# A retention and mixture-of-adapters kernel: the first half unit's scores moved into the last full unit, PSUM banks given to the state update first in the first chunk, one transposed key tile copied batch by batch

## The chip, the cores and the metric

The kernel runs on one core of a Trainium2 chip. The metric is the device time of one execution in microseconds. A core has five engines that work side by side and wait for one another through semaphores: TensorE (matrix products and transposes, its weight loads are listed apart in the profile), VectorE, ScalarE, GpSimd, and SyncE, which here issues most transfers. Matrix products land in PSUM, eight banks of which one holds 512 float32 values per partition.

## The reference, cut to what matters

Retention of 8 batches with 8 heads, sequence 576 and head dimension 64, then a mixture of 8 low-rank adapters of rank 16, of which each token uses two:

```
scores = scale * q @ k.T
out    = (scores * Dmat[h]) @ v          # Dmat = gamma_h ** (i - j) for j <= i, else 0
x      = out as (batch*seq, heads*64)    # 4608 x 512
logits = x @ w_gate; top 2 of 8, softmax weights w
result = x + sum over the two: w * (x @ A[e]) @ B[e]
```

## The kernel before, in words

The sequence is cut into four chunks of 128 positions and a last one of 64. A *unit* is one chunk of two batches: units 0 to 15 are full, 16 and 17 are the half chunk, each with four batches (two by two). Units 0 to 3 belong to the first chunk, which has no state from earlier chunks; from unit 4 on a state `P` (one tile for each pair of batches) carries the earlier chunks. The loads fetch four batches at a time (`q32`, `k32`, `v32`, three sets of buffers), so one load serves two units.

The work on a unit is split into stages, each a function:

- `stage_T` transposes q and k on TensorE into the PSUM tiles `pqT`, `pkT` (two each, one for each half of the positions) and copies them to `qT`, `kT` in SBUF, by VectorE in the first units and by ScalarE otherwise. `scale_k` then weights k in place on GpSimd (line 261).
- `stage_S` makes the scores, two PSUM tiles `ps` for each batch of a full unit, and VectorE multiplies each by the decay mask into `rt`. A half unit has two score tiles `pe` and results `rh`.
- `stage_Q` takes two tiles `px` and, where there is a state, adds `P` times `qT` into them. For a first-chunk unit it only takes the two banks and returns.
- `stage_U` forms the state update `pu` from k and v (32 matmuls recorded). VectorE makes `P` (first chunk) or `pn` out of it, and GpSimd then writes `P`.
- `stage_R` adds v times `rt` into `px`; VectorE scales the result into `xT`.
- `stage_Z` multiplies `xT` by the adapters and the gate into `pz`; VectorE copies the logits to `lg` and makes `ns`. `stage_V` runs the sigmoids `sg` on ScalarE (called by `stage_W` where it has not run), `stage_W` makes the weights `cm` and the weighted `zc` on VectorE and gives the bank of `pz` back.
- `stage_B` transposes `xT` back into two tiles `po`, `stage_X` transposes `zc` (`pzt`, copied to `zT`), and `stage_Y` adds the adapters' output to `po`, copies it to `osb` and stores it.

Three things set the order around the change. First, the matmuls, VectorE's and ScalarE's instructions are each chained in the order in which the stages are called (`chain`, lines 73 to 87, which is why nearly all of them carry line 81, 84 or 87 in the profile); GpSimd's and SyncE's are put in order by the framework. Second, the loop at the end (lines 607 to 708) interleaves stages of neighbouring units: a full unit t from 3 on runs S, T of unit t+1, W and B of unit t-1, Q, U, R, then X, Z and Y. Third, the PSUM banks are handed out by a queue:

```
def bank(shape, name, dtype=FP32):
    n = free.pop(0)
    ...
def done(*tiles):
    free.extend(held.pop(id(x))[0] for x in tiles)
```

A bank goes to the back of the queue when the *program text* gives it back, which may be right after the reading instruction was written down. A later tile that gets the same bank waits, at run time, until the last reader of the tile before it has finished. So the order in which `bank` is called decides which reader a tile waits for.

## Time and profile before

| | us |
|---|---|
| median of 4 runs | 195.03 |
| the runs | 195.12, 194.94, 194.85, 196.33 |
| time of the profiled execution | 195.12 |
| its span | 193.3 (mean granted TensorE clock 0.988) |
| TensorE matmuls busy | 180.6 |
| weight loads busy | 163.5 |
| VectorE busy | 110.4 |
| ScalarE busy | 72.0 |
| GpSimd busy | 58.8 |

A row of the timeline gives the start and the duration in microseconds, the engine (PE is TensorE's matmuls, PEld its weight loads, DVE VectorE, ACT ScalarE, POOL GpSimd), the line, the operation, "written tile <- read tiles", the shapes, how many instructions are merged into the row, and in brackets how long the engine had been idle and who the profile thinks released it. A matmul of float32 appears as two records, so a stage of 16 matmuls shows as 32. The releaser is inferred from semaphores; where an instruction waits for several, or where two engines signal at nearly the same time, the name can be wrong. A releaser "issue" means that the profile shows no wait.

### The profile page before, as it was taken

The numbers are of one execution on the slowest core, as the hardware profiler recorded it, in microseconds if no ns is written. First come the engines' busy times: TensorE is split into PE (matmuls) and PEld (weight loads), VectorE is DVE, ScalarE is ACT, GpSimd is POOL, SyncE is SP. The second block draws the span as 40 slices with busy tenths as digits, with TensorE's granted clock in tenths as the row PEclk, the third lists the DMA queues.
The fourth block names the chain that finished last, engine by engine and source line by source line (L and its number), as shares of the span: only waits on it lengthen the run. The fifth ranks groups of instructions, "written<-read, shape, count | busy, mean of one in ns | idle before, by whom it ended". The sixth has DMA issues, their size and how long they took to land. (4 is left out here: it accounts for less than half of the span.)

```text
span 193.3 us, 8113 instructions
## 1 busy us (share of the span) xinstructions
PE 180.6 (93%) x3612; PEld 163.5 (85%) x3612; DVE 110.4 (57%) x281; ACT 72.0 (37%) x195; POOL 58.8 (30%) x70
## 2 busy tenths in 40 slices
PE   7799997999999999979999999999999999988870
PEld 2598997989999999979999999999999999978750
DVE  4476956565656574744646564646474746453650
ACT  4111154262616170705252525344443435070440
POOL 8984026040424233330606051514242420200000
PEclk9999999999999999999999999999999999999995
DMA  6999978997998999696889898949980302020343
GB/s 138 266 242 251 288 221 234 249 300 216 254 369 252 240 335 270 172 283 225 231 242 304 264 259 229 251 110 244 186 209 1 114 3 112 3 112 3 112 109 109
DMA packets 53746, 38.73 MB, mean 200 GB/s; under 512 B 27472, under 2 KB 49104, under 8 KB 53712
## 3 DMA queue, kind: packets, MB, share of 16 engines
q1 hardware_dynamic: 52736, 37.75, 69.5%
q8 instruction: 28, 0.46, 1.0%
q10 hardware_dynamic: 832, 0.34, 0.6%
q0 software_dynamic: 144, 0.13, 0.4%
q14 instruction: 6, 0.05, 0.1%
HBM read 28.91 MB, written 9.44 MB: 198 GB/s over the span
## 5 line engine op out<-in xcount | busy, mean ns | idle before, releaser
L261 POOL TENSOR_TENSOR k<-k,pack 128x512 f32<-128x512 f32 x32 | 32.7, 1042 | 81.8 <-PE pkT L81 71.3
L84 DVE TENSOR_TENSOR rt<-ps,mask 128x512 f32<-128x512 f32 x64 | 41.0, 686 | 16.5 <-PE ps L81 15.7
L81 PE MATMUL pz<-AW,xT 128*128 128x136 f32 x288 | 37.4, 283 | 0.2 <-DVE xT L84 0.2
L81 PE MATMUL ps<-qT,kT 64*128 64x128 f32 x512 | 35.7, 281 | 0.9 <-DVE kT L84 0.9
L81 PEld LDWEIGHTS pz<-AW,xT 128*128 128x128 f32 x288 | 34.6, 190 | 0.6 <-DVE xT L84 0.5
L81 PEld LDWEIGHTS ps<-qT,kT 64*128 64x128 f32 x512 | 31.0, 188 | 4.0 <-PE po L81 2.7
L81 PE MATMUL px<-rt,v 128*64 128x128 f32 x512 | 31.0, 273 | 1.1 <-issue 1.1
L87 ACT COPY osb<-po 128x256 f32<-128x256 f32 x68 | 20.6, 386 | 28.4 <-PE po L81 28.0
L84 DVE TENSOR_TENSOR xT<-px,asc 128x512 f32<-128x512 f32 x36 | 24.6, 691 | 9.3 <-PE px L81 8.2
L81 PEld LDWEIGHTS px<-rt,v 128*64 128x64 f32 x512 | 27.9, 137 | 1.2 <-issue 1.2
L87 ACT COPY zT<-pzt 128x256 f16<-128x256 f16 (+1 forms) x19 | 6.9, 361 | 54.1 <-PE pzt L81 54.1
L87 ACT COPY kT<-pkT 128x512 f32<-128x512 f32 x33 | 17.9, 590 | 14.7 <-PE pkT L81 14.7
L395 POOL TENSOR_TENSOR P<-pn,gdec 128x512 f32<-128x512 f32 x12 | 15.3, 1272 | 25.5 <-DVE pn L84 22.6
L87 ACT COPY qT<-pqT 128x512 f32<-128x512 f32 x32 | 17.2, 590 | 8.3 <-PE pqT L81 8.3
L81 PE MATMUL pu<-v,k 128*64 128x64 f32 x512 | 18.4, 225 | 1.6 <-POOL k L261 1.1
L81 PEld LDWEIGHTS pu<-v,k 128*64 128x64 f32 x512 | 16.3, 138 | 4.1 <-issue 2.6
L84 DVE COPY lg<-pz 128x16 f32<-128x16 f32 (+1 forms) x19 | 3.3, 173 | 26.6 <-PE pz L81 26.6
L84 DVE TENSOR_TENSOR pn<-pu,P 128x512 f32<-128x512 f32 x12 | 8.3, 692 | 16.0 <-PE pu L81 16.0
L81 PE MATMUL px<-qT,P 64*64 64x128 f32 (+1 forms) x512 | 15.9, 262 | 0.6 <-issue 0.6
L81 PEld LDWEIGHTS px<-qT,P 64*64 64x64 f32 x512 | 12.7, 133 | 1.7 <-issue 0.7
L81 PE MATMUL po<-id,xT 64*128 64x64 f32 x288 | 12.7, 224 | 0.7 <-DVE zc L84 0.7
L81 PE MATMUL pkT<-id,k 64*128 64x64 f32 x288 | 12.4, 224 | 0.6 <-DMA k<-in_k_dram 0.5
(51 smaller groups left out, 149.6 us busy)
## 6 DMA issues: line engine op xcount, KB each, us to landing
out_dram<-osb SPq DMA_DIRECT2D x32, 256.0 KB, 3.1
q<-in_q_dram SPq DMA_DIRECT2D x4, 512.0 KB, 6.5
k<-in_k_dram SPq DMA_DIRECT2D x4, 512.0 KB, 7.2
v<-in_v_dram SPq DMA_DIRECT2D x4, 512.0 KB, 7.6
out_dram<-osb SPq DMA_DIRECT2D x6, 128.0 KB, 2.3
Arow<-in_moe_A_dram SPq DMA_DIRECT2D x1, 256.0 KB, 5.4
out_dram<-osb ACTq DMA_DIRECT2D x2, 128.0 KB, 2.7
Bcat<-in_moe_B_dram POOLq DMA_DIRECT2D x1, 128.0 KB, 4.7
```

The lines of the kernel that those rows point to most:

```text
L81: chain("pe", nc.tensor.matmul(*args, **kw))
L84: chain("dve", getattr(nc.vector, fn)(**kw))
L87: chain("act", getattr(nc.scalar, fn)(**kw))
L261: gp.tensor_tensor(out=kk[:, b], in0=kk[:, b], in1=gv[:, 0].unsqueeze(2).broadcast_to((128, H, Dh)), op=ALU.mult,)
L395: nc.gpsimd.tensor_tensor(out=Pt, in0=pn, in1=gdec, op=ALU.mult)
```

## The change

Three edits, and no instruction is added except two copies:

1. In the first chunk (units 0 to 3) `stage_U` is called before `stage_Q`. As `stage_Q` there only takes two banks, TensorE's order stays the same: U, then R. What changes is that `pu` now takes the first free bank and `px` the next two, where `px` took the first two and `pu` the third.
2. In unit 15, the last full one, `stage_S` of unit 16 is called between `stage_Q` of unit 15 and `stage_Q` of unit 16, where before it opened unit 16. TensorE runs Q(15), S(16), Q(16), U(15), R(15), X(14), Z(15), Y(14), and then goes straight on to the transposes of unit 17; VectorE makes `rh` of unit 16 before `pn` of unit 15. The banks of the tiles in between move with it: `pe` takes the banks that `px` of unit 16 took, `px` of unit 16 those of `pkT` of unit 16, `pu` of unit 15 that of the first `pe`.
3. In unit 0, `kT` is copied in four pieces, one for each half of the positions and each batch (ScalarE takes one half, VectorE the other), where it was two whole tiles. The scores of batch 0 then need only the first two pieces.

```diff
-                if t < 2 and nm == "qT" or t < 3 and nm == "kT" and g == 1:
+                if t == 0 and nm == "kT":
+                    for b in range(2):
+                        x = dst[:, b, :, rows(g)]
+                        if g == 1:
+                            vec("tensor_copy", out=x, in_=ps[g][:, :, b])
+                        else:
+                            act("copy", out=x, in_=ps[g][:, :, b])
+                elif t < 2 and nm == "qT" or t < 3 and nm == "kT" and g == 1:
                     vec("tensor_copy", out=o, in_=ps[g])
...
+            stage_U(0)
             stage_Q(0)
-            stage_U(0)
             stage_R(0)
...
+            stage_U(1)
             stage_Q(1)
-            stage_U(1)
             stage_R(1)
...
+            stage_U(2)
             stage_Q(2)
-            stage_U(2)
             scale_k(3)
             stage_R(2)
...
             stage_B(t - 1)
-            stage_Q(t)
+            if units[t][0] > 0:
+                stage_Q(t)
             if not is_full(t + 1):
+                stage_S(t + 1)
                 stage_Q(t + 1)
             stage_U(t)
             scale_k(t + 1)
+            if units[t][0] == 0:
+                stage_Q(t)
             stage_R(t)
...
-        stage_S(t)
         stage_W(t - 1)
         stage_T(t + 1)
```

## The prediction

> **What bounds the kernel now.** I read the page first (busy shares, slices, granted clock), then the timeline of TensorE with the idle time ahead of each group, then the waits and the neighbours of each hole. The chain that ended last covers only the last 2 us, so I don't use it.

> ```profile
> span 193.3 us, 8113 instructions
> ...
> PE 180.6 (93%) x3612; PEld 163.5 (85%) x3612; DVE 110.4 (57%) x281; ACT 72.0 (37%) x195; POOL 58.8 (30%) x70
> ...
> PEclk9999999999999999999999999999999999999995
> ...
> q8 instruction: 28, 0.46, 1.0%
> ```

> TensorE works 180.6 of 193.3 us at full clock; no other engine is near that. The program only gets shorter where TensorE stands still. The holes that the change can touch, from the timeline:

> ```profile
> 8.90 2.06 PE L81 MATMUL ps<-qT,kT 64*128 64x128 f32 x32 [0.91 <-DVE kT L84]
> ...
> 16.08 0.71 PE L81 MATMUL pkT<-id,k 64*128 64x64 f32 x16 [0.48 <-DMA k<-in_k_dram]
> ...
> 30.18 2.48 DVE L84 TENSOR_TENSOR rt<-ps,mask 128x512 f32<-128x512 f32 x4 [1.31 <-PE ps L81]
> ...
> 31.65 2.04 POOL L261 TENSOR_TENSOR k<-k,pack 128x512 f32<-128x512 f32 x2 [1.58 <-PE pkT L81]
> ...
> 32.77 1.15 PE L81 MATMUL pu<-v,k 128*64 128x64 f32 x32 [1.13 <-POOL k L261]
> ...
> 42.23 1.15 PE L81 MATMUL pu<-v,k 128*64 128x64 f32 x32 [0.47 <-DVE cm L84]
> ...
> 85.80 0.44 PE L81 MATMUL px<-rt,v 128*64 128x128 f32 x4 [1.07 <-issue]
> ```

> ```profile
> 161.59 1.07 ACT L87 COPY kT<-pkT 128x512 f32<-128x512 f32 x2 [0.36 <-PE pkT L81]
> ...
> 161.94 2.37 PE L81 MATMUL px<-qT,P 64*64 64x128 f32 x96
> ...
> 162.52 0.48 DVE L84 TENSOR_TENSOR zc<-pz,cm 128x128 f16<-128x128 f32 x2
> ...
> 169.52 1.20 ACT L87 COPY osb<-po 128x256 f32<-128x256 f32 x4 [1.75 <-PE po L81]
> 169.63 1.02 PEld L81 LDWEIGHTS pe<-qT,kT 64*64 64x64 f32 x64 [0.21 <-PE po L81]
> ...
> 170.57 0.52 ACT L87 ACTIVATE sg<-lg,ns 128x8 f32<-128x8 f32 x2
> ...
> 170.84 1.29 DVE L84 TENSOR_TENSOR rh<-pe,maskh 128x512 f32<-128x512 f32 x2 [0.90 <-PE pe L81]
> ...
> 172.05 0.35 DVE L84 SCALAR_TENSOR_TENSOR cm<-pz,m,sg 128x8 f32<-128x8 f32 x2
> ...
> 172.85 0.71 PE L81 MATMUL po<-id,xT 64*128 64x64 f32 x15 [0.39 <-DVE zc L84]
> ...
> 176.11 0.34 PE L81 MATMUL px<-qT,P 64*64 64x64 f32 x7 [0.60 <-issue]
> ```

> Between 45 and 160 us the only hole is the one at 85 us.

> **U first (units 0 to 3).** Walking the free list through the program tells whose bank each tile inherits. In unit 2, pu takes the bank of the fourth ps tile; its reader is the fourth rt operation, which ends at 32.66, and U starts at 32.73. The row names GpSimd's scaling, but that pair scales unit 3's k, and its second half ends at 33.69 while U's second head, which waits for its own k half, loads at 32.85: the named releaser cannot be it. After the change pu takes the second ps bank, free at 31.47 (second of four operations from 30.18; they start 0.60 apart and take 0.69). The last transpose of kT is issued at 31.41, so U starts near 31.54: 1.19 earlier. Behind it, R's px banks are the third and fourth ps (free at 32.07 and 32.66); R begins 0.93 after U (32.47), its second half at 33.36, so neither waits. VectorE must still do cm and zc (to 33.33) before P, so P ends and xT starts at 33.82 where R would have allowed 33.64; Z then starts at 34.57 instead of 35.67. **1.1 us.**
> In unit 3, pu inherits the fourth ps again (rt ends at 42.08, U starts 42.20); afterwards it inherits pqT of unit 4, copied by ScalarE until 40.97. B ends at 41.61, the hole goes: **0.53** (0.47 and 0.58 on the two rows of the hole). R's fourth-ps bank (42.08) is needed only at 43.5. Units 0 and 1 show no wait at U (12.03 and 20.76 follow their predecessors), so they get 0. From unit 4 on every tile inherits a bank of the same role as before.

> Is the 1.6 us kept? Only a landing could eat it. The tightest is the third k transfer, landed at 38.94, wanted at 40.48 before and at 39.38 after: 0.4 us of cover. The three batches of buffers let it be issued without a wait for TensorE, so it doesn't move; if it came 1.5 us later, unit 2's gain would be gone. The second v landed at 29.78, wanted at 31.54; later transfers have 6 us and more.

> **kT by batch (unit 0).** Pieces of 256 elements instead of 512: the osb copies of 128x256 took 386 ns on ScalarE and 420 on VectorE, kT itself 590 and 684. First pieces end at 8.49 instead of 8.76, so S starts 0.27 earlier; the second pieces (8.86 at the latest) are wanted at 9.57. [...] But the 0.27 is worth **0**: TensorE reaches unit 1's kT transposes that much earlier and stands before a k transfer that landed at 15.95 (row at 16.08; the hole grows from 0.48 to some 0.75). If that cover is gone, it is 0.27 gained; pieces that fail to overlap lose at most 0.2, also hidden. ScalarE's AW copies and VectorE's rt follow in the same shade.

> **S and Q of unit 16 inside unit 15.** No instruction is added: 32 matmuls (64 weight loads, 1.02 us) and two rh operations move up, no DMA with them. S follows Q(15) at 162.86; kT's second copy has ended (162.67), but pe1 inherits pz(14), whose last zc ends at 163.00. TensorE resumed at 163.12 at that point before too, for px1 of Q(16), so this wait only changes its tenant. S ends at about 164.2, Q(16) (0.95) at 165.15. pu(15) now inherits pe0: rh0 runs from 164.3 to 164.97, just hidden; cover gone costs up to 0.1. U(15), R, X, Z and Y come 0.92 later than before. VectorE's pn and xT queue behind rh, which is done at 165.6, before pn is due at 166.4. ScalarE's order is unchanged.
> After Y(14) S is no longer there, and T(17) starts at 170.55 instead of 170.72. Then B(15) waits for zc(15): before, sg was over at 171.09 but cm stood behind rh on VectorE until 172.05. Now sg, behind the osb copies on ScalarE, runs 171.49 to 172.01, and zc ends 1.15 us after sg's start (unit 16: 179.29 to 180.44), at 172.64 instead of 172.80. TensorE just waits longer at the same place. **0.16 gained**, of 1.0 us that moved; between -0.1 and 0.3.

> **Code loading.** TensorE's program arrives in packets of 16 KB (28 packets, row q8), 256 instructions of 64 bytes. Counting TensorE's records, the "issue" holes that end at 85.80 and 176.11 (the last start before them is at 84.46 and 175.29) stand at records 3008 and 6848, fifteen blocks of 256 apart; the packets ahead of them landed at 84.58 and 174.91, and both times TensorE went on 1.2 us after the landing. [...] I take 0, range 0 to 0.2 while the packet starts on time. The two holes, 1.3 and 0.8 us from start to start, I leave where they are.

> **Sum** against the profiled execution (span 193.33, time 195.12, so 1.8 around it): 1.1 + 0.53 + 0 + 0.16 = 1.8; span 191.5, time 193.3. The median of the runs is 0.09 lower, within the rounding: **193.3 us**.

> **Rivals.**
> Rival 1. The new timing loses another code block. A packet started 3.8 us late at 79.6 to 83.4, when the DMA engines were nearly full; five other blocks last only 4.1 to 5 us. One more hole of 1.3: 194.6. Against: before's runs at 194.85 to 195.12 agree; for: one stands at 196.33.
> Rival 2. The same the other way, the hole at 85 goes: 192.0.
> Rival 3. The k landing holds unit 4, or the bank is not what U(2) waits for: 1.1 lost, 194.4. The order of VectorE's ends speaks against.
> [...]

> **How the numbers follow.** Chances: forecast 0.60 (own range 192.8 to 193.9), rival 1 0.14, rival 2 0.13, rival 3 0.08, rival 4 0.05. A measurement of this kernel can tell about 0.5% (1 us) from no change: faster means below 194.05. Faster: 0.59 of the forecast, all of rival 2, 0.02 of rival 3: 0.74. Same: 0.13 of rival 1, the rest of rival 3, 0.01 of the forecast: 0.20. Slower: rival 4, and 0.01 of rival 1 (two blocks lost): 0.06. The range, 191.9 to 194.8, takes in rivals 1 to 3; rival 4 is left out.

> **What would show it.** The pu groups of units 2 and 3 without a hole; pkT of unit 1 with some 0.75 us ahead of it; pe between two px groups near 163 us less 1.6, the wait there still 0.25; po(15) with 1.0 to 1.3 us ahead of it, for zc. Wrong: U(2) still held; a new "issue" hole of over 1 us, above all at 165 less 1.6; po(15) resumed later than 172.85 less 1.6.

## The result: 0.4% faster, half of what was forecast

The changed kernel takes **194.1 us** (median of 43 runs, 192.49 to 196.79); the kernel before, run beside it, takes 194.85 us (64 runs). The ratio is **0.9959** [0.9942 to 0.9975]. The forecast was 193.3 us, 1.7 us below the 195.03 that was known then; some 0.8 us came. The measured time lies inside the range (191.9 to 194.8), outside the likeliest case's own range (192.8 to 193.9), and the gain is under the 0.5% that separates "faster" from "same". In a later comparison the same kernel stood at 0.9943 [0.9921 to 0.9964], 193.55 us.

The profiled execution took 193.65 us (before: 195.12), with a span of 191.9 us (193.3). The page of the changed kernel:

```profile
span 191.9 us, 8118 instructions
...
PE 181.1 (94%) x3612; PEld 163.7 (85%) x3612; DVE 110.4 (58%) x282; ACT 72.0 (38%) x196; POOL 58.8 (31%) x70
...
PEclk9999999999999999999999999999999999999995
...
q8 instruction: 28, 0.46, 1.0%
```

TensorE's work (3612 matmuls), its clock (0.990 granted, 0.988 before) and the code packets (28) are as before; only idle time can have moved. The timeline of the changed kernel (start, duration, engine, line, operation, tiles, form, count, and in brackets the idle time ahead with its releaser):

```profile
9.00 0.65 ACT L87 COPY kT<-pkT 128x256 f32<-128x256 f32 x2 [5.13 <-PE pkT L81]
9.04 0.76 DVE L84 COPY kT<-pkT 128x256 f32<-128x256 f32 x2 [0.95 <-PE pkT L81]
...
9.61 2.06 PE L81 MATMUL ps<-qT,kT 64*128 64x128 f32 x32 [0.64 <-DVE kT L84]
...
16.08 0.67 PE L81 MATMUL pkT<-id,k 64*128 64x64 f32 x16
...
31.53 1.15 PE L81 MATMUL pu<-v,k 128*64 128x64 f32 x32
...
40.61 1.15 PE L81 MATMUL pu<-v,k 128*64 128x64 f32 x32
...
50.56 1.15 PE L81 MATMUL pu<-v,k 128*64 128x64 f32 x32
...
64.99 1.09 PE L81 MATMUL pz<-AW,xT 128*128 128x136 f32 x8 [0.37 <-issue]
...
160.52 1.29 PE L81 MATMUL pe<-qT,kT 64*64 64x64 f32 x61
...
161.66 1.15 PE L81 MATMUL px<-qT,P 64*64 64x64 f32 x61
...
163.37 0.27 PE L81 MATMUL px<-qT,P 64*64 64x64 f32 x2 [0.57 <-issue]
163.57 1.15 PE L81 MATMUL pu<-v,k 128*64 128x64 f32 x32
...
169.91 0.52 ACT L87 ACTIVATE sg<-lg,ns 128x8 f32<-128x8 f32 x2
170.28 0.41 DVE L84 SCALAR_TENSOR_TENSOR cm<-pz,m,sg 128x8 f32<-128x8 f32 x2 [1.00 <-ACT sg L87]
170.61 0.48 DVE L84 TENSOR_TENSOR zc<-pz,cm 128x128 f16<-128x128 f32 x2
171.24 0.68 PE L81 MATMUL po<-id,xT 64*128 64x64 f32 x15 [0.85 <-DVE zc L84]
...
174.66 0.35 PE L81 MATMUL px<-qT,P 64*64 64x64 f32 x9 [0.85 <-issue]
```

The two `pu` rows of units 2 and 3 have no bracket any more. The `pe` row of unit 16 stands between two `px` groups. But there are three "issue" holes where before had two: the one ahead of 85.80 is gone, a small one has come at 64.99, and a new one at 163.37 stands inside Q(16), between the moved S(16) and U(15).

How far each point of TensorE's timeline moved against the kernel before:

| start of | before, us | after, us | moved | since the row above |
|---|---|---|---|---|
| kT transposes, unit 1 | 16.08 | 16.08 | 0.00 | |
| U(2) | 32.77 | 31.53 | -1.24 | hole gone |
| U(3) | 42.23 | 40.61 | -1.62 | 0.2 given back at Z(2), 0.5 hole gone |
| Y (first `po<-Bcat` row after 65 us) | 67.00 | 65.91 | -1.09 | new hole at 64.99 |
| Y (first such row after 85 us) | 88.21 | 85.82 | -2.39 | before's hole at 85.80 not there |
| U(15) | 164.23 | 163.57 | -0.66 | S(16) ahead of it (0.83), new hole 0.8 |
| transposes of q, unit 17 | 170.72 | 168.97 | -1.75 | S(16) no longer here |
| B(15), second part | 172.85 | 171.24 | -1.61 | waits for `zc` |
| end of Q(17)'s hole | 176.11 | 174.66 | -1.45 | that hole is 0.2 longer |
| end of the span | 193.3 | 191.9 | -1.4 | |

So the two `pu` waits and the `zc` step gave about what was forecast. The middle hole was 0.8 us shorter here than before; what is missing is the hole at 163.37.

TensorE's instruction records (weight loads, matmuls and semaphore instructions, 7289 before and 7292 after), counted from the start, show what the "issue" holes are. Each of them stands directly behind a record whose number leaves the remainder 192 when divided by 256. There are 28 such places in either trace and 28 code packets, of 16384 bytes each, so such a place is taken for the border between two code blocks of 256 instructions (which makes 64 bytes each). From the traces, for the two late holes of the changed kernel and for the same two borders in the kernel before (times in us):

```
kernel  previous border passed  packet for the next block  block used up  TensorE goes on
before  6080 at 162.77          162.93 to 163.86           166.85         no hole
before  6592 at 173.09          173.87 to 174.91           175.29         176.11
after   6080 at 160.41          161.13 to 162.09           162.59         163.37
after   6592 at 171.42          172.17 to 173.42           173.60         174.66
```

In these four the packet for the next block starts 0.16 to 0.78 us after TensorE has passed the border into the current one and takes 0.9 to 1.25 us, and in the three with a hole TensorE goes on 1.2 to 1.3 us after it has landed. Where a packet had landed 1.24 us or more before the current block was used up, as nearly all do, the traces of this case show no hole; where it was under 1.17 us, each of them shows one. The block from 6080 to 6336 took 4.1 us before; with S(16) moved into it, it is used up in 2.2 us. Its packet started 0.72 us after the border here, not 0.16.

### The profile page after: what moved, and what is told of

It is laid out like the page before. It is cut to its first block, busy times and chain, and to the rows that moved or that the text cites. A ratio compares the mean times of both kernels' runs of the same rounds, so it can differ in the third digit from the quotient of the medians.

```text
span 191.9 us, 8118 instructions
## 1 busy us (share of the span) xinstructions
PE 181.1 (94%) x3612; PEld 163.7 (85%) x3612; DVE 110.4 (58%) x282; ACT 72.0 (38%) x196; POOL 58.8 (31%) x70
## 5 line engine op out<-in xcount | busy, mean ns | idle before, releaser
L261 POOL TENSOR_TENSOR k<-k,pack 128x512 f32<-128x512 f32 x32 | 32.7, 1042 | 78.8 <-PE pkT L81 73.5
L84 DVE TENSOR_TENSOR rt<-ps,mask 128x512 f32<-128x512 f32 x64 | 41.0, 686 | 16.2 <-PE ps L81 16.2
L81 PE MATMUL pz<-AW,xT 128*128 128x136 f32 x288 | 37.6, 283 | 0.6 <-issue 0.4
L81 PE MATMUL ps<-qT,kT 64*128 64x128 f32 x512 | 35.7, 281 | 0.6 <-DVE kT L84 0.6
L81 PEld LDWEIGHTS pz<-AW,xT 128*128 128x128 f32 x288 | 34.7, 190 | 1.2 <-DVE xT L84 0.5
L81 PEld LDWEIGHTS ps<-qT,kT 64*128 64x128 f32 x512 | 31.0, 188 | 3.7 <-PE po L81 2.7
L87 ACT COPY osb<-po 128x256 f32<-128x256 f32 x68 | 20.6, 386 | 29.1 <-PE po L81 26.9
L81 PE MATMUL px<-rt,v 128*64 128x128 f32 x512 | 30.8, 273 | 0.0
L84 DVE TENSOR_TENSOR xT<-px,asc 128x512 f32<-128x512 f32 x36 | 24.6, 690 | 7.7 <-PE px L81 6.6
L81 PEld LDWEIGHTS px<-rt,v 128*64 128x64 f32 x512 | 27.8, 137 | 0.0
L87 ACT COPY zT<-pzt 128x256 f16<-128x256 f16 (+1 forms) x19 | 6.9, 361 | 52.5 <-PE pzt L81 52.5
L87 ACT COPY kT<-pkT 128x512 f32<-128x512 f32 (+1 forms) x34 | 18.0, 579 | 14.7 <-PE pkT L81 14.6
L87 ACT COPY qT<-pqT 128x512 f32<-128x512 f32 x32 | 17.2, 592 | 8.1 <-PE pqT L81 8.1
L84 DVE COPY lg<-pz 128x16 f32<-128x16 f32 (+1 forms) x19 | 3.3, 173 | 26.8 <-PE pz L81 26.8
L81 PE MATMUL pu<-v,k 128*64 128x64 f32 x512 | 18.5, 225 | 0.0
L81 PEld LDWEIGHTS pu<-v,k 128*64 128x64 f32 x512 | 16.3, 138 | 2.3 <-issue 1.9
L81 PE MATMUL px<-qT,P 64*64 64x128 f32 (+1 forms) x512 | 16.1, 261 | 1.4 <-issue 1.4
L84 DVE TENSOR_TENSOR pn<-pu,P 128x512 f32<-128x512 f32 x12 | 8.3, 692 | 15.2 <-PE pu L81 15.2
L81 PEld LDWEIGHTS px<-qT,P 64*64 64x64 f32 x512 | 12.7, 133 | 2.5 <-issue 1.7
L81 PE MATMUL po<-id,xT 64*128 64x64 f32 x288 | 12.6, 224 | 1.1 <-DVE zc L84 1.1
L81 PEld LDWEIGHTS pqT<-id,q 64*128 64x128 f32 x288 | 11.4, 143 | 1.4 <-POOL pick L141 0.8
```

The source lines that it names most:

```text
L81: chain("pe", nc.tensor.matmul(*args, **kw))
L84: chain("dve", getattr(nc.vector, fn)(**kw))
L87: chain("act", getattr(nc.scalar, fn)(**kw))
L261: gp.tensor_tensor(out=kk[:, b], in0=kk[:, b], in1=gv[:, 0].unsqueeze(2).broadcast_to((128, H, Dh)), op=ALU.mult,)
```

## The experiments

The theory: the parts of the change are worth what the sum says, except that S(16) beside Q(15) and Q(16) makes one code block so short that its successor is late. The rivals: the move of S costs through waits of banks or VectorE; the U-first part or the kT part is worth less than summed; or it is only the random place of the code holes. All ratios are to the kernel before, run on the same chip in the same comparison (194.54 us in the first, 194.5 in the second, 194.35 in the third); nothing of the computation is left out in any of these kernels.

**U first alone.** The kernel before, with only

```diff
+            stage_U(0)
             stage_Q(0)
-            stage_U(0)
...
+            stage_U(1)
             stage_Q(1)
-            stage_U(1)
...
+            stage_U(2)
             stage_Q(2)
-            stage_U(2)
...
-            stage_Q(t)
+            if units[t][0] > 0:
+                stage_Q(t)
...
             stage_U(t)
+            if units[t][0] == 0:
+                stage_Q(t)
```

> U first in units 0 to 3 alone. Theory (the three edits add up, U first keeps its 1.6 us, and the moved scores of unit 16 give back about 0.6 through a code block that lands too late): 1.6 us below the kernel before, ratio 0.992; U of units 2 and 3 without a hole, T of unit 4 some 1.6 us earlier. Rival (holes from code blocks in the crowded middle eat about half of whatever TensorE gains before them, and the moved scores cost nothing): 0.8 us, ratio 0.996.

Measured: 193.15 us (14 runs), **0.9923** [0.9898 to 0.9949], a gain of 1.5 us. The timeline has both groups without a hole:

```profile
32.29 1.15 PE L81 MATMUL pu<-v,k 128*64 128x64 f32 x32
...
41.37 1.15 PE L81 MATMUL pu<-v,k 128*64 128x64 f32 x32
```

The profiled execution is the longest of the 14 (195.77 us), with code holes at 66, 125 and 177 us, so only its rows ahead of these are read here. This part is worth what the sum said (1.6 us), and it is as large as or larger than the gain of the whole change. Something in the other two parts takes from it.

**S(16) moved, alone.** The kernel before, with only

```diff
+                stage_S(t + 1)
                 stage_Q(t + 1)
...
-        stage_S(t)
```

> Scores of unit 16 inside unit 15 alone. Theory: a new hole of about 0.8 us between S and U, where the code block ends, less the 0.16 gained at B of unit 15: 0.6 us above the kernel before, ratio 1.003. Rival (it costs nothing): 0.16 below, ratio 0.999.

Measured: 195.1 us (22 runs), **1.0029** [1.0004 to 1.0054]: 0.6 us slower, where the prediction had this part at 0.16 us faster. Its timeline:

```profile
163.94 1.15 PE L81 MATMUL px<-qT,P 64*64 64x64 f32 x62
...
165.92 0.27 PE L81 MATMUL px<-qT,P 64*64 64x64 f32 x1 [0.83 <-issue]
166.12 1.15 PE L81 MATMUL pu<-v,k 128*64 128x64 f32 x32
```

The hole comes with this part alone, at the same record, 6336. The border before it was passed at 162.70, the packet ran from 163.37 to 164.54, the block was used up at 164.87, and TensorE went on at 165.92.

**kT by batch, alone.**

```diff
+                if t == 0 and nm == "kT":
+                    for b in range(2):
+                        x = dst[:, b, :, rows(g)]
+                        if g == 1:
+                            vec("tensor_copy", out=x, in_=ps[g][:, :, b])
+                        else:
+                            act("copy", out=x, in_=ps[g][:, :, b])
-                if t < 2 and nm == "qT" or t < 3 and nm == "kT" and g == 1:
+                elif t < 2 and nm == "qT" or t < 3 and nm == "kT" and g == 1:
```

> kT of unit 0 in four pieces alone. Theory: S of unit 0 starts 0.27 us sooner after the transposes, and TensorE waits that much longer for the k transfer of unit 1: 0, ratio 1.000. Rival (the early gain is kept): 0.27 below, ratio 0.9986; too small to tell by time, so the hole ahead of unit 1's kT transposes decides: about 0.75 us by the theory, 0.48 by the rival.

Measured: 194.69 us (22 runs), **1.0000** [0.9977 to 1.0024]. The scores of unit 0 do start sooner after their transposes:

```profile
9.45 2.06 PE L81 MATMUL ps<-qT,kT 64*128 64x128 f32 x32 [0.64 <-DVE kT L84]
```

The hole is 0.64 us instead of 0.91. That the 0.27 us is lost again ahead of unit 1's kT transposes could not be read here: the first loads landed some 0.8 us later in this execution, and there was no wait at that place at all. The interval allows a gain of 0.27 us (0.14%) as well as none.

The three parts add up to 0.9923, 1.0029 and 1.0000, or -0.48% together; the whole change measured -0.41% and -0.57%. Within the intervals they add up, and the S part is the one that had the wrong sign.

**S(16) out of the dense block.** The changed kernel, with S(16) after R(15) instead of between Q(15) and Q(16). It stays ahead of X, Z and Y, so the `zc` step keeps its gain:

```diff
-                stage_S(t + 1)
                 stage_Q(t + 1)
             stage_U(t)
...
             stage_R(t)
+            if not is_full(t + 1):
+                stage_S(t + 1)
```

> The changed kernel, but with the scores of unit 16 behind R of unit 15 instead of between the two Q. The same work then leaves the code block that ends in the dense stretch 1.9 us longer. Theory: no hole between Q of unit 16 and U of unit 15, 1.7 us below the kernel before, ratio 0.991. Rival (the hole has another cause, such as the wait of pe on zc, or U on the bank of pe): a hole stays where pe is written, or comes back as a wait of equal size; ratio 0.995 to 0.996 as in the changed kernel.

Measured: 192.96 us (22 runs), **0.9917** [0.9896 to 0.9937]. The timeline:

```profile
159.64 2.36 PE L81 MATMUL px<-qT,P 64*64 64x128 f32 x96
161.93 1.15 PE L81 MATMUL pu<-v,k 128*64 128x64 f32 x32
...
164.76 1.16 PE L81 MATMUL pe<-qT,kT 64*64 64x64 f32 x64
...
170.69 0.68 PE L81 MATMUL po<-id,xT 64*128 64x64 f32 x15 [0.85 <-DVE zc L84]
...
174.12 0.34 PE L81 MATMUL px<-qT,P 64*64 64x64 f32 x8 [0.84 <-issue]
```

U(15) follows Q(16) without a hole: with U and R between Q and S, the block lasts 4.0 us (160.46 to 164.45), and no hole stands at its end. The old hole in Q(17) is still there, and this execution has another at 121 us. This tells the code block apart from the banks or VectorE only in part, since the order of the banks changes too. The next runs leave order and banks alone.

**The same order, other block borders.** Some warm-up matmuls at the head, which run on idle data while the first loads are under way, were replaced by more and shorter ones: 144 more TensorE instructions ahead of the first scores (a warm-up matmul has two, weight load and matmul; the page then counts 3684 of each instead of 3612), so that every later border falls elsewhere. First in the changed kernel:

```diff
-    def spin(n):
+    def spin(n, small=0):
...
+        for _ in range(small):
+            mm(spare[0:64, 0:64], lhsT=idle[:, 0:64], rhs=idle[:, 0:64], start=True, stop=True)
...
-            spin(10)
+            spin(5, 27)
...
-            spin(6)
+            spin(2, 40)
             stage_T(0, ("kT",))
+            spin(0, 14)
```

> The changed kernel with 144 more instructions on TensorE at the start: nine of the 16 wide spin products are replaced by 67 narrow ones of 64 columns, and 14 more stand before the first scores; together they should take no longer than the loads that TensorE waits for there. All that follows stands 144 places later against the borders of the 256-instruction blocks, so that the border leaves the dense stretch of unit 15 and that of Q of unit 17; the shortest block then lasts 3.5 us. Theory (holes where a block's code lands late): both late holes go, 0.8 and 0.85 us; 1.6 us below the changed kernel, ratio to the kernel before 0.988. Rival (the holes belong to the instructions there, not to the border): ratio stays at 0.996.

Measured: 191.27 us (6 runs), **0.9846** [0.9807 to 0.9886]. The stretch of the dense block and of Q(17) in its timeline:

```profile
162.02 1.15 PE L81 MATMUL px<-qT,P 64*64 64x64 f32 x63
163.10 1.15 PE L81 MATMUL pu<-v,k 128*64 128x64 f32 x32
...
170.76 0.68 PE L81 MATMUL po<-id,xT 64*128 64x64 f32 x15 [0.86 <-DVE zc L84]
...
172.35 1.11 PE L81 MATMUL px<-qT,P 64*64 64x64 f32 x64
173.40 0.28 PE L81 MATMUL pzt<-ident,zc 128*128 128x128 f16 x2
```

Order, banks and all waits of other engines are those of the changed kernel (the wait for `zc` is still 0.86), and every "issue" hole has gone, late ones and middle one. S(16) and Q(16) are now cut by a border at 161.84, into blocks of 3.5 and 3.3 us instead of one of 2.2, and the packets for the blocks after them land 1.69 and 1.24 us before these are used up. The groups of the page by operation say the same. In the changed kernel and then in this one, busy time, mean ns, idle time and releaser:

```profile
L81 PE MATMUL px<-qT,P 64*64 64x128 f32 (+1 forms) x512 | 16.1, 261 | 1.4 <-issue 1.4
```

```profile
L81 PE MATMUL px<-qT,P 64*64 64x128 f32 (+1 forms) x512 | 15.6, 261 | 0.0
```

So the cause is where the instructions lie in their blocks, not what they wait for, unless the new warm-up itself makes the rest faster; the run with 256 instructions below decides that.

The same shift in the kernel before (same edit):

> The same 144 instructions in the kernel before. Theory: it has one late hole at a border, in Q of unit 17 (0.8 us), which goes: ratio 0.996. The difference between this and the changed kernel with the same instructions is then the change without code blocks: 1.6 + 0.16 = 1.8 us, as the prediction's sum had it. Rival (the holes belong to the instructions): 1.000, and the difference stays near 0.8 us.

Measured: 193.19 us (13 runs), **0.9924** [0.9898 to 0.9949], more than the theory's 0.996. In its profile not only the hole in Q(17) but also the one at 85 us is absent, which the theory had left in place. `pu` of units 2 and 3 still wait, as they did:

```profile
33.28 1.15 PE L81 MATMUL pu<-v,k 128*64 128x64 f32 x32 [1.13 <-POOL k L263]
...
42.74 1.15 PE L81 MATMUL pu<-v,k 128*64 128x64 f32 x32 [0.48 <-DVE cm L84]
```

The medians of the two shifted kernels differ by **1.9 us** (193.19 and 191.27, the latter of 6 runs), their ratios by 0.0078, which is 1.5 us; in the two profiles, the stretch from the kT transposes of unit 1 to the end is 1.7 us shorter (175.1 and 173.4). There is no code hole in either, so 1.5 to 1.9 us is what the change is worth without them, and the sum of the prediction was 1.8.

**The wait for `zc` as well.** With S(16) behind R, and the sigmoids of unit 15 put ahead of the output copies on ScalarE, which are shared with VectorE:

```diff
-            stage_Y(t - 1)
+            if not is_full(t + 1):
+                stage_V(t)
+            stage_Y(t - 1, spread=not is_full(t + 1))
```

> The version with the scores of unit 16 behind R of unit 15, and in unit 15 the two sigmoids before the copies of the stored output on ScalarE, half of those copies on VectorE. Theory (B of unit 15 waits 0.85 us for zc only because the sigmoids stand behind four copies on ScalarE): zc comes about 0.9 us sooner and the hole ahead of B goes; 0.8 us below the same version without it, ratio to the kernel before 0.987. Rival (the hole moves on: the copies that free the banks of po then come later, or the code of Q of unit 17, which lands at a time of its own, makes TensorE wait there instead): half of it or nothing, ratio 0.990 to 0.992.

Measured: 193.06 us (15 runs), **0.9932** [0.9908 to 0.9957]; the theory's 0.987 is out. The hole ahead of `po` is gone, but:

```profile
169.75 0.71 PE L81 MATMUL pkT<-id,k 64*128 64x64 f32 x15 [0.65 <-ACT osb L87]
170.24 0.79 PE L81 MATMUL po<-id,xT 64*128 64x64 f32 x16
...
174.33 0.34 PE L81 MATMUL px<-qT,P 64*64 64x64 f32 x8 [1.39 <-issue]
```

The transposes of unit 17's k now wait 0.65 us for the output copy that was put back, whose bank they inherit. TensorE reaches B(15) 0.45 us sooner all the same (170.24 against 170.69 in the kernel without this edit), and loses it in the code hole of Q(17), which grows from 0.84 to 1.39 us. The packet there started at about the same time in both (171.96 and 171.82), so in this pair the gain ahead of it was no gain.

Both edits with the shift by 144 instructions:

> The early sigmoids and the 144 instructions at the start together. Theory: neither hole is left before or in Q of unit 17; 0.85 us for Q and 0.8 for B below the version with the scores behind R: ratio to the kernel before 0.983. Rival: as for the early sigmoids and for the shift; only what the shift alone gives, 0.987.

Measured: 191.4 us (6 runs), **0.9838** [0.9804 to 0.9872]: no code hole, and the 0.65 us at `pkT` remains. It cannot be told from the shift of the changed kernel alone (0.9846).

**How much shift.** If only the position in the block counts, a whole block more (256 instructions) must change nothing. The changed kernel with the warm-up of 2 wide and 62 narrow, 1 and 49, and 30 narrow matmuls:

> The changed kernel with 256 instructions more on TensorE at the start, one whole block, as narrower spin products (32 columns); all that follows stands against the borders as in the changed kernel itself. Theory (the borders make the holes, not the spins): the two late holes are back, between Q of unit 16 and U of unit 15 and in Q of unit 17, about 0.8 us each; ratio to the kernel before 0.996. Rival (more or narrower spins make the rest faster, wherever the borders are): 0.985, as with 144 instructions.

Measured: 194.36 us (14 runs), **1.0004** [0.9983 to 1.0024]. Both late holes are back:

```profile
161.94 1.15 PE L81 MATMUL px<-qT,P 64*64 64x64 f32 x61
163.90 0.27 PE L81 MATMUL px<-qT,P 64*64 64x64 f32 x2 [0.81 <-issue]
...
175.45 0.35 PE L81 MATMUL px<-qT,P 64*64 64x64 f32 x9 [1.10 <-issue]
```

They end at the same groups with the same counts left (x2 and x9) as in the changed kernel. The rival, that more narrow warm-up or more instructions help by themselves (0.985), is out. The kernel is even 0.6% slower than the changed one in the same comparison. Its two late holes are 0.5 us longer together than in the first profile of the changed kernel, but only 0.3 longer than in the second; and in this execution TensorE reached the kT transposes of unit 1 late (16.72 against 16.08 in the first), held by the k transfer. Why the median of 14 runs is slower was not found.

The changed kernel with 48 more instructions (8 wide and 8 narrow, 4 and 16, 4):

> The changed kernel with 48 instructions more at the start. By the changed kernel's trace the block in unit 15 then lasts 2.4 us where it lasted 2.2, and the one in Q of unit 17 3.8 where it lasted 2.2. Theory (a block whose packet starts 0.2 to 1.3 us after its border, takes 1.0 and is usable 1.2 later needs 2.4 to 3.5 us): the hole in Q of unit 17 goes, that in unit 15 stays between 0 and 1 us: ratio 0.991. Rival (only the number of instructions ahead matters, in proportion): a third of the gain of 144 instructions, 0.992, with both holes shorter by a third.

Measured: 191.57 us (6 runs), **0.9872** [0.9834 to 0.9910]; 0.991 stands at the edge of the interval, and the hole left over for unit 15 did not come. Not a third of the effect of 144, but most of it: there is no "issue" hole in its trace.

```profile
161.54 1.22 PE L81 MATMUL px<-qT,P 64*64 64x64 f32 x63
162.69 1.15 PE L81 MATMUL pu<-v,k 128*64 128x64 f32 x32
...
171.95 1.11 PE L81 MATMUL px<-qT,P 64*64 64x64 f32 x64
172.99 0.28 PE L81 MATMUL pzt<-ident,zc 128*128 128x128 f16 x2
```

The block with Q(17) now lasts 5.0 us (172.36 to 177.38). The dense one still lasts only 2.46 (159.65 to 162.11). It was covered in this execution because its packet started 0.16 us after the border and landed at 160.76, 1.35 before the end; with a start 0.7 us after it, as in the changed kernel, it would by estimate have cost some 0.5 us (159.65 + 0.7 + 0.96 + 1.3 against 162.11). By this the shift by 144 is the safer one, though the two times can't be told apart.

The changed kernel beside these two:

> The changed kernel itself, beside the two shifted ones on the same chip. Both theories: ratio 0.996, with holes of about 0.8 us at the same two places.

Measured: 193.55 us (22 runs), **0.9943** [0.9921 to 0.9964].

```profile
84.13 0.44 PE L81 MATMUL px<-rt,v 128*64 128x128 f32 x4 [0.54 <-issue]
...
164.57 0.27 PE L81 MATMUL px<-qT,P 64*64 64x64 f32 x2 [1.10 <-issue]
...
175.58 0.35 PE L81 MATMUL px<-qT,P 64*64 64x64 f32 x9 [0.56 <-issue]
```

The two late holes sit at the same records as in its first profile, with other lengths (1.10 and 0.56 against 0.57 and 0.85). The middle one is at 84 us, where before had it, not at 65: its place changes from execution to execution of the same kernel.

The fastest are the three without a code hole and with U first: the changed kernel shifted by 144 (191.27 us) or by 48 instructions (191.57), and the reordered one shifted by 144 (191.4). Their intervals overlap.

## Why the prediction was half right

**U first: right.** The banks that were walked through gave U(2) at 31.54 and Z(2) at 34.57; the trace has 31.53 and 34.60. U(3)'s hole of 0.53 went. Nothing landed late behind it. The part alone measured 1.5 us of the 1.6 summed. All profiles agree: from the kT transposes of unit 1 to U of unit 4 it is 36.1 us in the four kernels with the old order (before, S alone, kT alone, before shifted) and 34.5 in the nine with the new one (34.7 in one). In the kernel before, U of unit 4 started at

```profile
52.18 1.04 PE L81 MATMUL pu<-v,k 128*64 128x64 f32 x28
```

and in the changed one at 50.56, with the kT transposes of unit 1 at 16.08 in both.

**kT by batch: right as far as it shows.** The first piece let S start 0.27 us sooner (0.91 to 0.64), so what two pieces cost more than one copy decided nothing. That was also less than an estimate from the kernel before gives: two copies of 420 ns (`osb`, 128x256) against one of 684 (`kT`, 128x512) are 0.16 us more on VectorE, while the two pieces took 0.76 us where one copy took 0.69, 0.07 more. Whether the 0.27 is lost again at unit 1's k, as was argued, is not shown: the sign named for it, 0.75 us ahead of unit 1's kT transposes, did not come (no wait there in the first profile, 0.17 in the second), as the first loads landed later. The time of the part alone (1.0000) leaves room for both.

**S(16) moved: the waits were right.** S follows Q(15), `pu` does not wait for `rh`, T(17) and B(15) follow as worked out; the wait for `zc` is 0.85, a little under the 1.0 to 1.3 that was named for it. The gain of 0.16 there is best read in the shifted kernel, where no hole disturbs it: against its own shift at the last Y before Q(15), U(15) is 0.83 us later and R(16) 0.15 earlier than in the kernel before. The move takes 0.83 us where 0.92 was summed.

**The dense block: the term that was mis-sized.** The sum has nothing for it: "I take 0, range 0 to 0.2 while the packet starts on time." No run shows that 0 for the block as the change makes it, of 2.2 us; the hole at its end was 0.8 us in the changed kernel's profile (162.59 to 163.37), 1.05 in the S part alone, 1.3 in the second profile of the changed kernel. The place (163.4) and the delay after landing (1.2 us) came as forecast; the number that failed is the packet's start. In the kernel before, the packet of this block started 0.16 us after the border at 162.77 and landed at 163.86; 1.2 us later is 165.06, against 165.0 for the end of a block of 2.2 us: next to nothing to add. That start was taken from one packet of one execution. In the nine profiles with unmoved borders (the shift by 256 among them) the same packet started 0.16 us after it twice, 0.67 to 0.72 three times and 1.07 to 1.36 four times. The block lasts 2.2 us, and a start of 0.7, a packet of 1.0 and 1.2 to 1.4 after it need 3. At the next border of the same trace (173.09 to 173.87) the delay was 0.78; with that row in place of the other, the working would have given a hole of 0.6, and a sum of 1.2 instead of 1.8. This was rival 4 in small: it has the packet of this block late, by 1.8 us before the gain is gone, and was given 0.05. That packets after 139 us start within 1 us, as was held against it, misread the trace: the one at 139.67 started 1.16 us after its border, and the one at 177.33 started 1.2 us after TensorE had gone on at 176.11.

That the borders cost time in this kernel is shown by moving them: 48 instructions take the changed kernel from 0.9943 to 0.9872, 144 take it to 0.9846 in another comparison, and a whole block (256) gains nothing (1.0004).

**Rivals 1 and 2: both happened, and they are one.** In the first profile the hole at 85 us went and one of 0.5 us came at 64.99; in the second it was at 84.13. It was wrong to reckon with the middle hole as a fixed property of the code's timing.

**The sum, closed.** In the profiled pair: 1.0 and 0.5 at the two `pu`, 0.05 carried from unit 0's loads, 0.15 at `zc`, 1.3 for the hole at 85, less 0.5 at 65, 0.8 in the dense block and 0.2 in Q(17): 1.5 of a measured 1.4. If the middle hole and the length of the one in Q(17) are left out as chance, 1.7 less 0.8 is 0.9, and the medians differ by 0.8.

**What stays open.** What sets a packet's start was not found: past 150 us, with the loads over, it lies between 0.65 us before its border and 1.40 us after TensorE went on from it. Traffic alone does not decide it: where the other DMA queues were almost idle around the border, the traces still have starts from 0.5 us before to 1.4 us after it. It was not tried whether a packet can be made to start earlier. No code hole is left after a shift of 48 or 144 in any of four profiles, not even in the middle, where the packets start up to 4.3 us after their border among the loads; why the middle hole goes too was not tested by itself (one profile with unmoved borders, that with 256 instructions, had none there either).

## To carry to other kernels

Before matmuls are moved next to each other, count TensorE's instructions in the blocks of 256 that they fall in: here blocks used up in 2.2 us left TensorE idle for the next one, and some dozens of harmless instructions in an idle stretch at the head, which moved the borders, were worth more (0.7 to 1.0% of the time) than the change itself (0.4 to 0.6%). Which shift helps has to be measured: 256 brought the late holes back. Walking the free list of PSUM banks to the reader that a tile really waits for predicted starts to within 0.05 us (31.54 and 34.57 against 31.53 and 34.60), where the profile's releaser named the wrong engine. A delay that a verdict rests on is not to be taken from a single event: the same trace held another with five times its size.
